# New order lists for both ends of a fused attention and adapter kernel

## The chip, the cores and the metric

The kernel runs on one core of one Trainium2 chip. The metric is the time of one execution on the device in microseconds. The profile is of one further execution; its span counts from the first to the last instruction. Five engines work in parallel[...]: TensorE (PE: matmuls and transposes), VectorE (DVE), ScalarE (ACT: exp, tanh, copies), GpSimd (POOL) and SyncE (SP: issues DMA transfers).[...]

## The reference: what is computed

For each of 4 batches, 12288 queries of 128 channels attend to 768 keys. The keys are 4 x 4 means of a 384 x 32 image, times a weight matrix, and serve as values too. Each of the 49152 output rows then gets a top-2 mixture of 8 low-rank adapters (rank 16).

```python
B, C, Hh, Ww = (4, 128, 384, 32)
kv_pool = kv.reshape(B, H // r, r, W // r, r, C).mean(axis=(2, 4))   # r = 4
k = v = kv_pool.reshape(B, -1, C) @ w_sr
s = (q @ k.transpose(0, 2, 1)) / np.sqrt(C)
a = np.exp(s - s.max(-1, keepdims=True)); a /= a.sum(-1, keepdims=True) + 1e-09
x = (a @ v).reshape(B * S, D)
logits = x @ w_gate                        # 8 experts, the two largest kept
for e in range(E):                         # w: softmax over the two kept logits
    z = x[mask] @ A[e]; delta[mask] += w[mask, k, None] * (z @ B[e])
return x + delta
```

## The kernel before: the parts concerned

The 49152 queries are 96 chunks of 512 (`T`), 24 per batch. The 768 keys of a batch are six tiles of 128, handled in three blocks `h` of two tiles. A chunk goes through these stages, named as in the order lists:

```python
def scores(k, r):       # "sc k r": one third of the keys: 2 matmuls of 512 columns on PE, 1 exp on ACT
    ps = ps_s.tile([P, 2, T], FP32, tag="sg", name="sg")            # PSUM, 2 buffers of 2 banks
    for i in range(2):
        mm(ps[:, i], kfT[b][:, 2 * r + i], rhs, start=True, stop=True)
    keep(nc.scalar.activation(em[k][:, 2 * r:2 * r + 2], ps, AF.Exp, bias=0.0, scale=scale))

def attend(k, s):       # "at k s": 128 queries against all keys: 6 matmuls of 137 columns into acc
    acc[k] = ps_a.tile([P, S, 256], FP32, tag="acc", name="acc")    # PSUM, 1 buffer of 2 banks
    for j in range(J):
        mm(o, em[k][:, j, s * P:(s + 1) * P], vx[b][:, j], start=(j == 0), stop=(j == J - 1))

def normalize(k):       # "nm k": DVE, reciprocal and product of all 4 x 136 columns
# "tp k": DVE, 4 maxima;  "ro"/"ga": GpSimd and one tanh on ACT, the gates of the experts
# "tt kx kh V|A": PE transposes x of chunk kx and the gated h of chunk kh, one copy on DVE or ACT
# "dn k": PE, x times A (4 matmuls);  "ge k": DVE, h times gates;  "up k": PE, times B (4 matmuls)
# "fi k": DVE adds x, SP stores 256 KB
# "ca k" / "pd k": instead of "fi", ACT copies the sum out of PSUM and GpSimd adds x
# tail forms with PSUM of their own choice: xt, cx (transpose x, copy), hb, ht, ch (the same of h),
# dn2, ge2, db, up2, af (add and store); a pair "0 2" or "2 4" means half a chunk
```

`ps_m` ("mb") holds everything else in PSUM: 2 buffers of one bank. `keep(...)` fixes the program order. The first loads and the preparation of the first batch:

```python
keep(nc.scalar.dma_start(w_sr_sb, w_sr))
keep(nc.scalar.dma_start(w_gate_sb, moe_w_gate))
load_q(0, 0, GC * S)                       # 1 MB: queries of chunks 0 to 3
for h in range(3):                         # 6 MB: keys, 24 transfers of 256 KB
    for r in range(4):
        for x in range(2):
            load_kv(0, h, r, x)
for m in range(GC):
    load_q(1, m * S, m * S + S)            # 4 x 256 KB: queries of chunks 4 to 7
...
def pair_step(h, r, x):                    # "ad": DVE adds two of the four image rows
    u, v = (kvr[b, h][:, r + i, x] for i in range(2))
    keep(adder.tensor_tensor(u, u, v, op=ALU.add))
# "ky h half": PE transposes the 16 sums of the block in fp32, adding them up in PSUM;
#              DVE scales by 1/16.  "k2 h": times w_sr -> keys kfT.  "va h": values vx.
# "tq g m e":  the first 8 query chunks are transposed on PE (fp32), 4 transposes and a copy
def first_casts(watch):                    # "cs1": GpSimd waits for the last query load, then starts
    keep(nc.gpsimd.tensor_copy(late, watch))   # the casts of later queries in DRAM
    for g in range(2, 4):
        cast_q(g)
```

Chunks 0 to 13 follow a list written out, chunks 14 to 71 a regular slot, and chunks 72 to 95 a second list:

```python
def slot(k):
    ...
    o.append(f"sc {k} 0")
    o += [f"nm {k - 2}", f"tt {k - 6} {k - 7} V", f"sc {k} 1", f"up {k - 8}", f"fi {k - 8}",
          f"at {k - 1} 0", f"tp {k - 2}"]
    o += [f"sc {k} 2", f"dn {k - 6}", f"ge {k - 6}"]
    o += [f"at {k - 1} {s}" for s in range(1, S)]
```

The head list begins "ad 0 0; tq 0 0 A; ad 0 1; ad 0 2; cs1; tq 0 1 A; ad 0 3; ky 0 0; ...". In the tail list the slot's order goes on, with the open stages of older chunks brought in two at a time between chunks 72 and 78. From chunk 93 on the half forms are used.

Of the kernel before, what the change touches and what calls it, by code (L numbers as in the profile page):

```python
# [20 lines left out]
def kernel(  # L21
# [10 lines left out]
    nc = tc.nc  # L32
# [74 lines left out]
    def turn_q(g, m, engine):  # L107
        if g not in qT:
            qT[g] = qpool.tile([P, GT], BF16, tag="qT", name="qT")
        ps = mtile([P, S, P], name="qT_ps")  # L110
        for i in range(S):
            mm(ps[:, i], q_f[g][:, m * S + i], id_f, is_transpose=True,
               start=(i == 0), stop=(i == S - 1))
        o = qT[g][:, m * T:(m + 1) * T].rearrange("p (s t) -> p s t", s=S)
        if engine is nc.scalar:
            keep(nc.scalar.copy(o, ps))
        else:
            keep(nc.vector.tensor_copy(o, ps))
# [6 lines left out]
    load_q(0, 0, GC * S)  # L125
    for h in range(3):
        for r in range(4):
            for x in range(2):
                load_kv(0, h, r, x)
    for m in range(GC):  # L130
        load_q(1, m * S, m * S + S)
    b_f = const.tile([P, C], FP32)
    keep(nc.sync.dma_start(b_f, moe_B.rearrange("e r c -> (e r) c")))
    a_f = const.tile([P, P], FP32)
    keep(nc.sync.dma_start(a_f, moe_A.rearrange("e c r -> c e r")))


    warm = const.tile([P, 1], FP32)
    nc.vector.memset(warm, 0.0)
    keep(nc.scalar.activation(warm, warm, AF.Exp, bias=0.0, scale=1.0))  # L140
    id_f = const.tile([P, P], FP32)
    make_identity(nc, id_f)
    id_bf = const.tile([P, P], BF16)
    nc.vector.tensor_copy(id_bf, id_f)
    wext = const.tile([P, VC], FP32)
    nc.vector.tensor_copy(wext[:, 0:C], w_sr_sb)
    wT_ps = mtile([P, C], name="wT_ps")
    mm(wT_ps, w_sr_sb, id_f, is_transpose=True, start=True, stop=True)
    wT = const.tile([P, C], FP32)
    nc.vector.tensor_copy(wT, wT_ps)  # L150
    w2_ps = mtile([P, E], name="w2_ps")
    mm(w2_ps, wT, w_gate_sb, start=True, stop=True)
    nc.vector.tensor_copy(wext[:, C:VC], w2_ps)


    kfT, vx = {}, {}

    def prepare(b, adder):
# [3 lines left out]
        def pool_step(h, step, lo, hi):  # L162
            t = kvr[b, h]
            if step < 3:
                u, v = t[:, 0].rearrange("p g c -> p (g c)"), t[:, step + 1].rearrange("p g c -> p (g c)")
            else:
                w = 2 * C if step == 3 else C
                u, v = t[:, 0, :, 0:w], t[:, 0, :, w:2 * w]
                keep(adder.tensor_tensor(u, u, v, op=ALU.add))
                return  # L170
            keep(adder.tensor_tensor(u[:, lo:hi], u[:, lo:hi], v[:, lo:hi], op=ALU.add))  # L171

        def pair_step(h, r, x):
            u, v = (kvr[b, h][:, r + i, x] for i in range(2))
            keep(adder.tensor_tensor(u, u, v, op=ALU.add))

        for h in range(3):
            if adder is nc.vector:
                sums.append([lambda h=h, r=r, x=x: pair_step(h, r, x)
                             for r in (0, 2) for x in range(2)])  # L180
                continue
# [5 lines left out]
        def keys(h, half=None):  # L187
            if h == 0 and half != 1:
                st["kpT"] = prep.tile([P, J, P], FP32, tag="kpT", name="kpT")
                kfT[b] = per_b.tile([P, J, P], BF16, tag="kfT", name="kfT")  # L190
            kpT = st["kpT"]
            if half != 1:
                st["ps"] = mtile([P, 2, P], name="kpT_ps")
            ps = st["ps"]
            if adder is nc.vector:
                parts = [(r, i, c) for r in (0, 2) for i in range(2) for c in range(4)]
            else:
                parts = [(0, i, 0) for i in range(2)]
            for n, (r, i, c) in enumerate(parts):
                if half is not None and r // 2 != half:  # L200
                    continue
                mm(ps[:, i], kvr[b, h][:, r, i, c * C:(c + 1) * C], id_f, is_transpose=True,
                   start=(n == 0), stop=(n == len(parts) - 1))
            if half == 0:
                return
            keep(nc.vector.tensor_scalar(kpT[:, 2 * h:2 * h + 2], ps, 1.0 / 16.0, None,
                                         op0=ALU.mult))

        def keys2(h):
            kpT = st["kpT"]  # L210
            ps = mtile([P, 2, P], name="kfT_ps")
            mm(ps, w_sr_sb, kpT[:, 2 * h:2 * h + 2], start=True, stop=True)
            keep(nc.vector.tensor_copy(kfT[b][:, 2 * h:2 * h + 2], ps))  # L213

        def values(h):
# [7 lines left out]
            if adder is not nc.vector:  # L223
                st["vb", h] = prep.tile([P, 2, C], BF16, tag="vb", name="vb")
                keep(nc.vector.tensor_copy(st["vb", h], ps[:, :, 0:C]))
# [8 lines left out]
        for h in range(3):  # L234
            for f in (keys, keys2, values) if adder is nc.vector else (keys, values, turn):
                rest.append(lambda h=h, f=f, **how: f(h, **how))
# [17 lines left out]
    def attend(k, s):  # L254
        b = k // NB
        if k not in acc:
            acc[k] = ps_a.tile([P, S, 256], FP32, tag="acc", name="acc")
        o = acc[k][:, s, 0:VE]
        for j in range(J):
            mm(o, em[k][:, j, s * P:(s + 1) * P], vx[b][:, j], start=(j == 0), stop=(j == J - 1))  # L260
# [11 lines left out]


# [16 lines left out]
    def route(k0):  # L290
        n = size[k0] * S
        eng = nc.gpsimd if k0 > 1 else nc.vector
# [74 lines left out]
    def bank(pool):  # L367
# [20 lines left out]
    def turn_x(k, pool):  # L388
        xT[k] = quad(bank(pool).bitcast(BF16), pool)
        xb = xn[k].bitcast(U16)[:, :, 1::2].bitcast(BF16)  # L390
        for s in range(S):
            mm(xT[k][:, s // 2, s % 2], xb[:, s, 0:C], id_bf, is_transpose=True,
               start=(s % 2 == 0), stop=(s % 2 == 1))

    def copy(engine, o, i):
        keep(nc.scalar.copy(o, i) if engine == "A" else nc.vector.tensor_copy(o, i))  # L396

    def fetch_x(k, engine):
        sb = run.tile([P, S, P], BF16, tag="tt1", name="tt1")
        copy(engine, four(sb), xT[k])  # L400
        xT[k] = sb
# [3 lines left out]
    def hold_h(k, pool):  # L405
        hps[k] = quad(bank(pool).bitcast(BF16), pool)

    def turn_h(k, lo=0, hi=S):
        for s in range(lo, hi):
            mm(hps[k][:, s // 2, s % 2], hg[k][:, s], id_bf, is_transpose=True,  # L410
               start=(s % 2 == 0), stop=(s % 2 == 1))

    def fetch_h(k, lo=0, hi=S, engine="A"):
        if lo == 0:
            hgT[k] = run.tile([P, S, P], BF16, tag="tt1", name="tt1")
        copy(engine, part(four(hgT[k]), lo, hi), part(hps[k], lo, hi))

    def hold_acc(k, pool="sg"):
        acc[k] = bank(pool)
# [3 lines left out]
    def attend_part(k, lo, hi):  # L423
        for s in range(S):
            for j in range(lo, hi):
                mm(acc[k][:, s, 0:VE], em[k][:, j, s * P:(s + 1) * P], vx[k // NB][:, j],
                   start=(j == 0 and s % 2 == 0), stop=(j == J - 1 and s % 2 == 1))

    def down_into(k, pool):
        hp[k] = quad(bank(pool), pool)  # L430
        for s in range(S):
            mm(hp[k][:, s // 2, s % 2], xT[k][:, s], a_bf, start=(s % 2 == 0), stop=(s % 2 == 1))

    def gate_part(k, lo, hi):
        if lo == 0:
# [3 lines left out]
        keep(nc.vector.tensor_tensor(  # L439
            part(four(hg[k]).rearrange("p a b (e r) -> p a (b e) r", e=E), lo, hi),  # L440
            part(four(hp[k]).rearrange("p a b (e r) -> p a (b e) r", e=E), lo, hi),
            part(g4, lo, hi).unsqueeze(3).broadcast_to([P, (hi - lo) // 2, 2 * E, RK]), op=ALU.mult))

    def hold_d(k, pool):
        dp[k] = quad(bank(pool), pool)

    def up_part(k, lo, hi):
        for s in range(lo, hi):
            mm(dp[k][:, s // 2, s % 2], hgT[k][:, s], b_bf, start=(s % 2 == 0), stop=(s % 2 == 1))
# [5 lines left out]
    def add_here(k, lo, hi, queue="SP"):  # L455
        osb = opool.tile([P, S, C], FP32, tag="osb", name="osb")[:, 0:hi - lo]
        keep(nc.vector.tensor_tensor(osb.rearrange("p (a b) c -> p a b c", b=2),
                                     part(four(dp[k]), lo, hi),
                                     part(four(xn[k][:, :, 0:C]), lo, hi), op=ALU.add))
# [57 lines left out]
    def plan(b):  # L517
        if b not in plans:
            plans[b] = prepare(b, nc.gpsimd if b else nc.vector)
# [3 lines left out]
        "tq": lambda g, m, e: turn_q(g, m, nc.scalar if e == "A" else nc.vector),  # L523
        "ad": lambda h, i: plan(0)[0][h][i](),
        "ky": lambda h, half: plan(0)[1][3 * h](half=half),
        "k2": lambda h: plan(0)[1][3 * h + 1](),
        "va": lambda h: plan(0)[1][3 * h + 2](),
        "cs": lambda: first_casts(kvr[0, 2][:, 3, 1, 0:1]),
        "cs1": lambda: first_casts(q_f[1][:, GC * S - 1, 0:1]),
# [10 lines left out]
        "xt": turn_x, "cx": lambda k, e="A": fetch_x(k, e), "hb": hold_h, "ht": turn_h, "ch": fetch_h,  # L540
        "o95": hold_acc, "pt": attend_part, "dn2": down_into, "ge2": gate_part,
# [4 lines left out]
    def follow(order):  # L546
        for item in order.replace("\n", " ").split(";"):
            what, *at = item.split()
# [31 lines left out]
ad 0 0; tq 0 0 A; ad 0 1; ad 0 2; cs1; tq 0 1 A; ad 0 3; ky 0 0; tq 0 2 V; ky 0 1; k2 0; ad 1 0; va  # L580
0; sc 0 0; tq 0 3 A; lq 2; sc 2 0; ad 1 1; ad 1 2; ad 1 3; ky 1 0; sc 1 0; ky 1 1; ad 2 0; sc 3 0;
k2 1; ad 2 1; va 1; sc 3 1; ad 2 2; sc 0 1; ky 2 0; sc 2 1; ad 2 3; kv 1 0 0; ky 2 1; sc 1 1; k2 2;
tq 1 0 V; sc 0 2; va 2; cab; sc 4 2; tq 1 1 V; at 0 2; kv 1 0 1; sc 1 2; at 0 1; sc 4 0; at 0 0; at
# [89 lines left out]
```

## Time and profile before

| | us |
|---|---|
| time, median of 3 | 393.8 (393.69 to 394.21) |
| span of the profiled execution | 392.3 |
| PE busy | 376.4 |
| VectorE busy | 325.3 |
| ScalarE busy | 298.0 |
| GpSimd busy | 205.0 |

The page's part 5 gives the durations of the main pieces (line, engine, operation, output<-input, shape and count; then busy us and mean ns of one; then the idle time of the engine just before them and what ended it):

```profile
L252 ACT ACTIVATE em<-sg 128x1024 f16<-128x1024 f32 x288 | 280.9, 1023 | 75.6 <-PE sg L68 74.7
L268 DVE TENSOR_TENSOR xn<-acc,rinv 128x544 f32<-128x544 f32 x95 | 68.8, 725 | 3.3
L349 DVE TENSOR_TENSOR hg<-h_ps,gw 128x512 bf16<-128x512 f32 x93 | 64.2, 690 | 7.0 <-PE h_ps L68 0.2
L335 DVE COPY tts<-tt_ps 128x1024 bf16<-128x1024 bf16 (+1 forms) x93 | 61.6, 663 | 2.6 <-PE tt_ps L68 1.6
L362 DVE TENSOR_TENSOR osb<-d_ps,xn 128x512 f32<-128x512 f32 x89 | 61.2, 690 | 0.0
```

Matmuls overlap in PE's pipeline, so their mean ns (379 for a score matmul) is longer than the distance from one to the next; that distance has to be read from the timeline or from the chain of waits.

### The profile page before, as it was taken

The page shows a single profiled execution, that of the slowest core. Times are in us where ns is not written, and L with a number is a line of the kernel's source. Part 1 is how long each engine was busy: PE and PEld are TensorE (multiplying, and loading weights), DVE is VectorE, ACT ScalarE, POOL GpSimd, SP SyncE. Part 2 cuts the span into 40 slices and gives each one's busy share as a digit, 9 for nine tenths or more (in the row PEclk, how much of TensorE's full clock was granted, in tenths as well). Part 3 has the DMA queues.
Part 4 walks back from the last instruction along what each step waited for, and adds up shares of the span by engine and source line. Part 5 has one row for each costly group of instructions (what it writes and reads, how often), then busy time and mean ns, then how long its engine had stood idle before and what let it go on. Part 6 is the DMA issues. An engine that isn't in the chain of part 4 may idle for free.

```text
span 392.3 us, 11714 instructions
## 1 busy us (share of the span) xinstructions
PE 376.4 (96%) x4589; PEld 302.3 (77%) x4589; DVE 325.3 (83%) x950; ACT 298.0 (76%) x375; POOL 205.0 (52%) x473
## 2 busy tenths in 40 slices
PE   3999999999999999999999999999999899999993
PEld 2767878888887888878888878888786678878882
DVE  2666769989888889888988988989887888888885
ACT  2378988787687787787777877877788787877873
POOL 0010479998331778587432677877524235444443
PEclk9999999999999999999999999999999999999997
DMA  8998969974596989885489999957644566573213
GB/s 296 367 266 222 210 237 245 264 173 136 140 304 145 298 206 342 183 190 135 108 217 256 297 257 295 187 139 134 156 142 110 154 157 148 144 159 105 79 60 136
DMA packets 71464, 76.47 MB, mean 195 GB/s; under 512 B 49936, under 2 KB 50704, under 8 KB 70928
## 3 DMA queue, kind: packets, MB, share of 16 engines
q1 hardware_dynamic: 70272, 63.98, 56.4%
q0 software_dynamic: 704, 11.54, 17.1%
q8 instruction: 36, 0.59, 0.6%
q10 hardware_dynamic: 432, 0.20, 0.2%
q14 instruction: 20, 0.16, 0.1%
HBM read 50.53 MB, written 36.70 MB: 222 GB/s over the span
## 4 chain that ended last, share of the span: by engine, by line
PE 85%; DMA 5%; SPq 3%; DVE 3%; POOL 2%; issue 1%; ACT 1%; ACTq 0%; DVEq 0%; POOLq 0%
PE acc L68 33%; PE sg L68 29%; PE tt_ps L68 10%; PE h_ps L68 5%; PE d_ps L68 5%; SPq L98 3%; DMA qT<-qbf 2%; DMA w_sr_sb<-in_w_sr_dram 1%; DMA kvr<-in_kv_dram 1%; PE v_ps L68 1%; PE kpT_ps L68 1%; DVE tts L335 1%; POOL kvr L171 1%; DVE xn L268 1%; ACT tt L396 0%
## 5 line engine op out<-in xcount | busy, mean ns | idle before, releaser
L252 ACT ACTIVATE em<-sg 128x1024 f16<-128x1024 f32 x288 | 280.9, 1023 | 75.6 <-PE sg L68 74.7
L68 PE MATMUL sg<-qT,kfT 128*128 128x512 bf16 x576 | 170.4, 379 | 0.4 <-DVE kfT L213 0.2
L68 PE MATMUL acc<-vx,em 128*128 128x137 f16 x2280 | 168.1, 223 | 0.0
L68 PEld LDWEIGHTS <-em 128*128 128x128 f16 x2304 | 146.1, 98 | 3.1 <-DVE xn L268 1.1
L68 PEld LDWEIGHTS <-tts 128*128 128x128 bf16 x740 | 56.1, 98 | 43.9 <-issue 2.8
L171 POOL TENSOR_TENSOR kvr<-kvr 128x512 f32<-128x512 f32 x54 | 67.5, 1274 | 13.1 <-DVE tts L335 13.1
L268 DVE TENSOR_TENSOR xn<-acc,rinv 128x544 f32<-128x544 f32 x95 | 68.8, 725 | 3.3
L349 DVE TENSOR_TENSOR hg<-h_ps,gw 128x512 bf16<-128x512 f32 x93 | 64.2, 690 | 7.0 <-PE h_ps L68 0.2
L335 DVE COPY tts<-tt_ps 128x1024 bf16<-128x1024 bf16 (+1 forms) x93 | 61.6, 663 | 2.6 <-PE tt_ps L68 1.6
L362 DVE TENSOR_TENSOR osb<-d_ps,xn 128x512 f32<-128x512 f32 x89 | 61.2, 690 | 0.0
L299 POOL TENSOR_TENSOR over<-xn,srt 128x64 f32<-128x64 f32 (+1 forms) x116 | 30.4, 283 | 56.0 <-DVE srt L286 56.0
L313 POOL TENSOR_TENSOR gw<-th,over 128x64 f32<-128x64 f32 (+1 forms) x58 | 17.0, 294 | 64.0 <-ACT th L311 63.7
L68 PEld LDWEIGHTS <-kfT 128*128 128x128 bf16 x576 | 45.6, 98 | 2.9 <-DVE kfT L213 1.0
L264 DVE RECIPROCAL rinv<-acc 128x4 f32<-128x4 f32 x95 | 17.4, 183 | 35.1 <-PE acc L68 34.5
L68 PEld LDWEIGHTS <-xn 128*128 128x128 bf16 x384 | 28.9, 98 | 20.0 <-DVE xn L268 0.4
L68 PE MATMUL d_ps<-b_bf,tts 128*128 128x128 bf16 x364 | 35.1, 219 | 1.6 <-DVE tts L335 1.1
L68 PE MATMUL h_ps<-a_bf,tts 128*128 128x128 bf16 x372 | 36.0, 219 | 0.3 <-ACT tts L333 0.3
L68 PE MATMUL tt_ps<-id_bf,xn 128*128 128x128 bf16 x372 | 35.8, 219 | 0.0
L68 PE MATMUL tt_ps<-id_bf,hg 128*128 128x128 bf16 x368 | 35.6, 219 | 0.0
L286 DVE MAX8 srt<-xn 128x8 f32<-128x8 f32 x380 | 34.3, 154 | 0.0
L68 PEld LDWEIGHTS <-hg 128*128 128x128 bf16 x384 | 25.8, 98 | 1.7 <-issue 0.4
L305 POOL TENSOR_SCALAR over<-over 128x64 f32<-128x64 f32 (+1 forms) x58 | 19.5, 336 | 5.3
(83 smaller groups left out, 208.5 us busy)
## 6 DMA issues: line engine op xcount, KB each, us to landing
out_dram<-osb SPq DMA_DIRECT2D x94, 256.0 KB, 3.6
kvr<-in_kv_dram SPq DMA_DIRECT2D x36, 512.0 KB, 6.1
qbf<-in_q_dram POOLq DMA_DIRECT2D x22, 512.0 KB, 6.2
kvr<-in_kv_dram SPq DMA_DIRECT2D x24, 256.0 KB, 5.1
qf<-in_q_dram SPq DMA_DIRECT2D x1, 1024.0 KB, 5.1
qf<-in_q_dram SPq DMA_DIRECT2D x4, 256.0 KB, 5.3
out_dram<-osb SPq DMA_DIRECT2D x3, 128.0 KB, 2.3
qT<-qbf SPq DMA_TRANSPOSE x22, 5.5
```

Of the source, the lines that this page charges most:

```text
L68: return keep(nc.tensor.matmul(*a, **k))
L171: keep(adder.tensor_tensor(u[:, lo:hi], u[:, lo:hi], v[:, lo:hi], op=ALU.add))
L252: keep(nc.scalar.activation(em[k][:, 2 * r:2 * r + 2], ps, AF.Exp, bias=0.0, scale=scale))
L264: keep(nc.vector.reciprocal(ri, acc[k][:, :, VC]))
L268: keep(nc.vector.tensor_tensor(x, acc[k][:, :, 0:VC], ri.unsqueeze(2).broadcast_to([P, S, VC]), op=ALU.mult))
L286: keep(nc.vector.max(srt[k0][:, m, s], xn[k][:, s, C:VC]))
L299: keep(eng.tensor_tensor(d, lg, so[:, :, i].unsqueeze(2).broadcast_to([P, n, 8]), op=ALU.subtract))
L305: keep(eng.tensor_scalar(mask, mask, 0.0, None, op0=ALU.is_ge))
L313: keep(eng.tensor_tensor(w[:, 0:n], th, mask, op=ALU.mult))
L335: keep(nc.vector.tensor_copy(sb[:, lo:hi], ps[:, lo:hi]))
L349: keep(nc.vector.tensor_tensor(hg[k].rearrange("p s (e r) -> p (s e) r", e=E), hp[k].rearrange("p s (e r) -> p (s e) r", e=E), gw[k0][:, m ...
L362: keep(nc.vector.tensor_tensor(osb, dp[k], xn[k][:, :, 0:C], op=ALU.add))
```

## The change

It changes what runs before chunk 14 and after chunk 71; the slot between is kept. Its aims: the first keys are loaded ahead of the queries, so that scores can begin sooner. PE multiplies zeros until data comes[...]. Both ends follow new lists in which scores run further ahead and late stages are cut into halves or go to another engine. Where two halves of a PSUM tile lie in different banks, the dependence between them is dropped.

```diff
-    load_q(0, 0, GC * S)
-    for h in range(3): ... load_kv(0, h, r, x)          [cut: 24 transfers of 256 KB]
-    for m in range(GC):
-        load_q(1, m * S, m * S + S)
+lkv 0 1 -; lkv 0 0 -; lf 1 1 2; lkv 0 3 -; lkv 0 2 -; lf 0 0 2; lf 0 2 4; lkv 1 2 -; lkv 1 3 -; lkv
+1 0 -; lkv 1 1 1; lkv 1 1 0; lkv 2 3 -; lkv 2 2 -; lkv 2 0 0; lkv 2 1 0; lkv 2 0 1; lkv 2 1 1; lf 1
+2 3; lf 1 0 1; lf 1 3 4; lab
     [lkv h r x: keys, "-" is a whole row set of 512 KB; lf g lo hi: query chunks; lab: adapters]
+    idle = const.tile([P, T], BF16)
+    keep(nc.vector.memset(idle, 0.0))
+    def spin(n):
+        ps = mtile([P, T], name="spin_ps")
+        for i in range(n):
+            mm(ps, idle[:, 0:P], idle, start=True, stop=True)
+    spin(11)
     [the weights' first steps move into weights(), "init" in the list]
+    def use(key, lo, hi, inst):
+        ...
+                tc.declare_no_dep(inst.ins, other.ins, reason="other PSUM bank")
+    def turn_k(h, half, x):               # "ky h half x": 4 transposes of a summed pair,
+        rows = [2 * half] if (h, 2 * half, x) in summed else [2 * half, 2 * half + 1]   # else 8
     [7 pair sums in the list instead of 12; "kc" scales, on ACT or DVE; k2, va, tq likewise]
+    def normalize_half(k, h):             # "nh k h": one bank's reciprocal and product
+    def attend_part(k, lo, hi):           # "pt k lo hi": keys lo..hi of all 512 queries, as exps come
-        eng = nc.gpsimd if k0 > 1 else nc.vector
+        eng = nc.gpsimd
-        "cs1": lambda: first_casts(q_f[1][:, GC * S - 1, 0:1]),
+        "cs": lambda w: first_casts(q_f[1][:, 15, 0:1]),
     [head list, its beginning]
+kb 1 mb; kb 0 sg; init; ad 0 2; ky 0 0 1; ky 0 0 0; tq 1 1 V mb; db 1 sg; ky 0 1 1; cs k; xb 3 mb;
+ky 0 1 0; kb 2 mb; kc 0 A; tq 0 0 A acc; tq 0 1 A sg; k2 0 sg A; lq 2; tq 0 2 V mb; tq 0 3 V mb; ad
+1 2; va 0 acc A; sc 5 0; kv 1 0 0; sc 0 0; ad 1 1; ky 1 1 1; ky 1 1 0; sc 1 0; sc 3 0; ky 1 0 0; ky
+1 0 1; ad 2 3; pt 0 0 2; ad 2 2; kc 1 A; ad 2 0; k2 1 mb A; ad 2 1; sc 2 0; va 1 mb V; sc 5 1; ky 2
+1 1; sc 1 1; ky 2 1 0; sc 3 1; ky 2 0 0; sc 0 1; ky 2 0 1; kv 1 0 1; kv 1 0 2; kc 2 V; tq 1 2 A mb;
+sc 2 1; k2 2 mb V; sc 6 1; va 2 mb V; kv 1 0 3; sc 0 2; tq 1 3 V mb; pt 0 2 4; sc 3 2; pt 0 4 6; sc
+1 2; tq 1 0 A mb; xb 1 mb; sc 2 2; nm 0; pt 1 0 2; hb 0 mb; ...
     [tail list, its end]
+95 acc; at 94 2; at 94 3; ch 90 0 2 A; ch 90 2 4 A; ga 93; db 92 acc; tt - 89 A; at 94 0; ge2 91 0
+4; at 94 1; hd 95 mb; tp 95; tt 92 - A; nh 94 1; nh 94 0; ro 95; dn2 93 0 4; ht 88 0 4; ge2 93 0 4; ...
+af 91 0 4 SP; af 92 0 2 SP; af 92 2 4 ACT; af 95 0 4 SP; db 94 acc; up2 94 0 4; fi 94
     [10 output adds of the tail go by "ca" and "pd" instead of 2; most attends go by parts ("pt")]
```

## The prediction

> **What bounds the kernel now.** I read the page's first two parts first (busy shares, then the 40 slices), then the chain of waits, then stage windows, and last the timeline of both ends.
>
> ```profile
> PE 376.4 (96%) x4589; PEld 302.3 (77%) x4589; DVE 325.3 (83%) x950; ACT 298.0 (76%) x375; POOL 205.0 (52%) x473
> PE   3999999999999999999999999999999899999993
> PEclk9999999999999999999999999999999999999997
> DMA  8998969974596989885489999957644566573213
> ```
>
> The reader is to see that TensorE (PE) is full from the second slice to the last but one, at full granted clock. Only the ends can give time back. How full it is inside comes from the cadence of the chain of waits:
>
> ```profile
> 324.33 1.08 PE acc L68 x18
> 327.96 1.08 PE acc L68 x18
> 331.59 1.08 PE acc L68 x18
> ```
>
> One chunk of 512 queries passes every 3.63 us. The pieces between are 1.44 us of attend (24 matmuls, 0.060 each), three score pairs of 0.43, 0.45 of transposes, and 0.22 each for down and up; they sum to 3.62 us. So the middle has no idle PE, and 96 x 3.63 = 348.5 of the 392.3 us are pure throughput. The rest is what the ends and the key preparation cost. The stage windows (start:end, length, then busy us and instructions of PE, PEld, DVE, ACT, POOL, clock, DMA share, GB/s) show where:
>
> ```profile
> 6.00:15.00 9.00, 7.88 (x39) 6.79 (x40) 5.32 (x12) 1.17 (x2) 0.00 (x0) 1.00 1.02 369
> 15.00:26.10 11.10, 10.48 (x64) 6.86 (x63) 7.32 (x16) 8.25 (x9) 0.42 (x2) 1.00 1.00 347
> 26.10:40.00 13.90, 13.90 (x152) 11.00 (x153) 9.15 (x38) 12.06 (x14) 0.97 (x2) 1.00 0.90 216
> ...
> 290.00:320.00 30.00, 28.10 (x356) 21.92 (x354) 24.48 (x65) 23.98 (x32) 10.68 (x40) 1.00 0.52 132
> 320.00:380.00 60.00, 60.00 (x767) 48.45 (x765) 52.19 (x151) 48.73 (x66) 26.21 (x104) 1.00 0.46 125
> 380.00:392.30 12.30, 6.16 (x82) 4.72 (x78) 7.40 (x26) 5.56 (x14) 4.40 (x10) 0.81 0.30 110
> ```
>
> Until 26.1 us the DMA share is 1.0: the 8.4 MB of first loads bind. From 320 to 380 PE does 767/60 = 12.8 matmuls per us; from 290 to 320 only 356/30 = 11.9, so 30 - 356/12.8 = 2.2 us are lost there; after 380, 82/12.8 = 6.4 us of work take 12.3. The timeline of the start gives the cold clock and the moment from which PE is full:
>
> ```profile
> 9.21 1.97 PE L68 MATMUL kpT_ps<-id_f,kvr 128*128 128x128 f32 x8
> ...
> 15.39 1.02 ACT L252 ACTIVATE em<-sg 128x1024 f16<-128x1024 f32 x1 [5.38 <-PE sg L68]
> ...
> 16.06 1.04 PE L68 MATMUL kpT_ps<-id_f,kvr 128*128 128x128 f32 x8
> ...
> 22.23 1.42 DVE L175 TENSOR_TENSOR kvr<-kvr 128x512 f32<-128x512 f32 x2 [0.54 <-DMA kvr<-in_kv_dram]
> ...
> 24.88 0.70 PE L68 MATMUL kfT_ps<-kpT,w_sr_sb 128*128 128x256 f32 x2
> ...
> 26.10 0.60 PE L68 MATMUL sg<-qT,kfT 128*128 128x512 bf16 x2
> ```
>
> The same eight fp32 transposes took 1.97 us at 9.2 and 1.04 at 16.1. The third key block's data is there at 22.2 to 22.9, and its scores start at 26.10. The window 26.1:40 contains 26 score matmuls (5.6 us), 96 attends (5.8), 14 small bf16 ones (0.8) and 16 fp32 ones (1.9): 14.1 us for 13.9. So PE is truly full from 26.1 on. **The head costs whatever steady work is still undone at that moment.**
>
> [...]The trace's 128 KB stores land 2.3 us after issue, the 256 KB ones after 3.6 under load. [...]The trace: an add of 512 columns takes 0.69 us, one of 256 columns 0.41.[...]
>
> **Part 1: order of the first loads.** Before, 1 MB of queries goes ahead of the keys. After, two of the four row sets of the first key block, a 256 KB query chunk (chunk 5), the other two rows, and then the 1 MB. The first block is complete after 2.25 MB instead of 3 MB, about 0.75 MB/0.39 = 2 us sooner (rate: 380 to 393 GB/s in the saturated 2 us windows). But before the last key piece stand 7.25 MB instead of 7.0: 0.65 us later. Set against this are whole-row transfers (one 0.6 us issue for 512 KB instead of 0.65 per 256 KB, where the rate dipped to 334 to 356), perhaps 0.5 us, and one pair sum instead of two after the last piece, 0.7. I expect the third key block's scores at 26.3 to 27.0, so about where they were. The watch of the query casts is the same last query column as before: nothing.
>
> **Part 2: spin.** 11 matmuls of 512 columns at the cold rate (2 x 0.215 = 0.43) are 4.7 us, from about 1.2 to 5.9, before w_sr lands (6.0 before). It costs nothing and makes the first transposes 0.11 apart instead of 0.22: 28 of them save 3 us of PE time in a stage where data binds. Alone it is worth little at the end.
>
> **Part 3: head list.** PE work listed ahead of the first third-block score (0.11 per fp32 transpose, 0.45 per query turn, 0.65 per key projection, 0.5 per value projection, 0.43 per score pair): before 48 transposes 5.3 + 5 turns 2.25 + 3 projections 2.0 + 2 values 1.0 + 8 pairs 3.45 + weights 1.0 = 15 us. After: 68 transposes 7.5 (five pair sums fewer on VectorE, 20 transposes more on PE) + 6 turns 2.7 + 2.0 + 3 values 1.55 + 11 pairs 4.7 + one attend part 0.5 + 1.0 = 20 us. Steady work moved ahead of the point: 3 pairs 1.3 + 1 turn 0.45 + 1 value 0.5 + 0.5 = 2.7 us. From this go the later point (0.2 to 0.9) and ScalarE: its six second-block exps can start only near 21.5 and run 0.93 to 1.0 apart plus a 0.59 query copy, so the score buffers (two) free up about 0.5 us late. Net head gain 2.7 - 0.7 - 0.6 = 1.4 us.
>
> **Part 4: tail list and halves.** From the middle's end (291 us) both lists do the same matmuls, about 95 us by the rates above. VectorE, by the row durations: before 26 normalizes 23.5, 25 maxima 9.1, 24 double copies 16.6, gates 20.9, adds 21.0, the rest 1.2 = 92.3 us. After: 17 whole and 18 half normalizes 25.8, maxima and late routes 12.9, copies 14.1, gates 21.2, adds 15.7 = 89.7, because ten output adds go through ScalarE (copy 0.59) and GpSimd (1.27). ScalarE rises from about 78 to 86 us (72 exps at 0.93, 26 tanh at 0.12, some 30 copies), which still fits. Scores run several chunks ahead (seven em buffers), so PE should not hit the 2.2 us of stalls at 290 to 320, where the catch-up doubled VectorE's work. At the very end it is the other way round: after the last attend, before had 11 groups of four matmuls (2.5 us) and 6.9 us to the last add. After, 20 groups (4.5 us) and on VectorE two half normalizes 1.2, maxima 0.7, 4 gates 2.8, eight adds 5.0 (one chunk in halves) = 9.7 us. The last attend thus comes 2.2 + 2.0 us sooner and is followed by 2.8 us more: +1.4. If VectorE's total counts (2.6 less), up to +3. The last store has 256 KB and a full add, -0.5. I take +2.6 - 0.5 = 2.1 us, plus 0.5 for finer bank waits.
>
> **Sum.** 1.4 + 2.1 + 0.5 = 4.0 us of 393.8: 389.8 us.
>
> **Rivals.** (a) Nearly nothing: the head stays bound by the 8.4 MB, whose last key piece comes 0.65 us later, and the tail turns PE stalls into a VectorE backlog. For it: the DMA share of 1.0 up to 25 us, and 9.7 us of VectorE work behind the last attend; 392.5 to 394. (b) Near the ideal: PE full from 6 us to the end. All PE work is 348.5 + 7.7 (key preparation of three batches, 9 steps each at about 0.28 us, by the slots of 3.74 to 4.15 us in the chain) + 15.6 (the first batch: 7.5 + 8 turns 3.6 + 2.0 + 1.55 + 1.0) = 371.8 (rounded); + 6 at the start + about 5 at the end = 383. For it: the middle shows that such lists hold PE at 100%. Against it: 20 us of work ahead of a point at 26.5 leave 0.5 us of slack. I would give it 386 at best. (c) Slower: a fixed order on in-order engines, with long runs through one acc buffer and score buffers lent to gates, meets a late cast or transposed load, and stalls stack up; 395 to 398. Against it: the list before was of the same kind and ran without PE idle from 26 to 70.
>
> **Range and chances.** Head 0 to 2.7, tail 0 to 4.5: the range is 386.6 to 393.0. Over 2% means below 385.9, which needs (b) nearly whole: 0.10. Slower by over 2% means above 401.7: 0.02. The rest, 0.88, within 2%.
>
> **What would show it.** First exp at 13 to 14 us instead of 15.4; transposes 0.11 apart from the start; the first third-block score near 26.5 and PE full after it. In the window 290:320 PE back at 12.8 matmuls per us. At the end, VectorE nearly without gaps after the last attend while PE has them. I am wrong if the first third-block score comes later than 27.5 (rival a), if PE shows gaps between 27 and 70 (c), or if the time from the last attend to the end is under 10 us although seven chunks' adds are open (b).

## The result, and the profile after

| | before | after |
|---|---|---|
| time, median of 4 | 393.76 us (393.69 to 394.21) | 388.93 us (388.78 to 389.29) |
| span of the profiled execution | 392.3 us | 387.5 us |

The ratio of the times is 0.9876, with a 95% interval of 0.9859 to 0.9893: 1.2% faster, 4.8 us. The prediction was 389.8 us (386.6 to 393.0).

From the page of the changed kernel, busy time of each engine and two of the 40-slice rows:

```profile
PE 378.9 (98%) x4620; PEld 303.8 (78%) x4620; DVE 313.5 (81%) x973; ACT 308.3 (80%) x401; POOL 211.0 (54%) x474
...
PE   7899999999999999999999999999999999999994
...
DMA  7998997975596999985579989856745665532245
```

VectorE has 12 us less to do than before, ScalarE 10 us and GpSimd 6 us more. PE has 2.5 us more, in a span 4.8 us shorter. In the PE row, the 7 in the first slice is mostly the zeros.

The stage windows of the changed kernel (start:end, length, then busy us and instructions of PE, PEld, DVE, ACT, POOL, clock, DMA share, GB/s):

```profile
6.00:15.00 9.00, 7.24 (x60) 6.47 (x59) 2.76 (x6) 1.84 (x5) 0.00 (x0) 1.00 1.02 388
15.00:26.10 11.10, 10.78 (x78) 7.89 (x76) 5.15 (x10) 9.63 (x13) 0.06 (x1) 1.00 0.94 348
...
290.00:320.00 30.00, 30.00 (x350) 22.80 (x348) 22.61 (x86) 29.20 (x38) 9.60 (x31) 1.00 0.59 124
...
380.00:387.50 7.50, 2.46 (x32) 1.73 (x30) 3.94 (x8) 2.31 (x5) 0.85 (x3) 0.87 0.66 247
```

The DMA share is still about 1 up to 26 us, so the first loads fill the queues as before. But PE does 138 instructions between 6 and 26.1 us instead of 103. Between 290 and 320 us PE no longer idles at all. After 380 us only 32 matmuls are left (82 before), and the DMA share of that stretch is 0.66 instead of 0.30: what is left is mostly stores.

The timeline of the head of the changed kernel (start, duration, engine, line, operation, output<-input, shape, count; in brackets the idle time before it and what ended it):

```profile
6.93 1.95 PE L68 MATMUL sg<-id_f,kvr 128*128 128x128 f32 x16
...
10.74 0.69 DVE L195 TENSOR_TENSOR kvr<-kvr 128x512 f32<-128x512 f32 x1 [3.46 <-DMA kvr<-in_kv_dram]
...
15.33 1.94 ACT L319 ACTIVATE em<-sg 128x1024 f16<-128x1024 f32 x2
...
24.20 0.69 DVE L195 TENSOR_TENSOR kvr<-kvr 128x512 f32<-128x512 f32 x1 [0.56 <-DMA kvr<-in_kv_dram]
...
27.64 0.59 PE L68 MATMUL sg<-qT,kfT 128*128 128x512 bf16 x2
```

Row by row: the first 16 transposes take 1.95 us. The last rows of the first key block are there at 10.74. The first exp starts at 15.33 (15.39 before). The last key piece is there at 24.20 (22.2 to 22.9 before), and the first third-block score starts at 27.64 (26.10 before). So the first exp did not move, and the third-block score moved back by 1.5 us. These marks differ from one execution to the next: in seven traces with this head, this one among them, the first exp starts between 14.74 and 15.65, the third-block score between 27.11 and 28.00.

Where the time went is read from a mark that both kernels share. The first two key transposes of batch 1 stand in the unchanged middle, in the slot of chunk 14 (tile view; after the count come the durations in ns, min/median/max, then the first and last start in us). Before:

```profile
L68 PE MATMUL kpT_ps<-id_f,kvr x2: 273/276/280, 70.3 to 70.4; 128*128 128x128 f32 x2
```

After:

```profile
L68 PE MATMUL kpT_ps<-id_f,kvr x2: 272/277/282, 69.3 to 69.4; 128*128 128x128 f32 x2
```

The changed kernel passes it 1.05 us sooner (unrounded starts). The last key preparation of the middle comes at 284.4 instead of 285.5, so the middle gave nothing. **In these two executions 1.05 of the 4.8 us come from the head and 3.75 from the tail.** The seven traces with this head and the bank rule pass the mark between 68.7 and 69.6, the two with the head of before at 70.1 and 70.3. So the head's share is about 1 us, and a difference of some tenths between two single traces says nothing.

The end of the changed kernel, in the timeline (SPq is the engine that issues the stores):

```profile
375.34 0.88 PE L68 MATMUL acc<-vx,em 128*128 128x137 f16 x12
...
380.84 3.65 SPq L554 DMA_DIRECT2D out_dram<-osb  x5
...
383.45 0.69 DVE L551 TENSOR_TENSOR osb<-acc,xn 128x512 f32<-128x512 f32 x1
```

The last attend ends at about 376.2. Before, the last attend matmuls were these, and ended at 382.2:

```profile
381.56 0.64 PE L68 MATMUL sg<-vx,em 128*128 128x137 f16 x8
```

From the last attend to the end it takes 11.3 us instead of 10.1.

### The profile page after: what moved, and what is told of

Same layout as the page of the kernel before. It is cut to its first block, busy times and chain, and to the rows that moved or that the text cites. A ratio compares the mean times of both kernels' runs of the same rounds, so it can differ in the third digit from the quotient of the medians.

```text
span 387.5 us, 11812 instructions
## 1 busy us (share of the span) xinstructions
PE 378.9 (98%) x4620; PEld 303.8 (78%) x4620; DVE 313.5 (81%) x973; ACT 308.3 (80%) x401; POOL 211.0 (54%) x474
## 4 chain that ended last, share of the span: by engine, by line
PE 82%; DMA 8%; POOL 5%; DVE 1%; ACT 1%; issue 1%; SPq 0%; POOLq 0%; DVEq 0%; ACTq 0%
PE acc L68 32%; PE sg L68 29%; PE tt_ps L68 8%; DMA kvr<-in_kv_dram 6%; PE h_ps L68 4%; PE d_ps L68 3%; PE tail_ps L68 3%; DMA qT<-qbf 2%; POOL osb L562 1%; PE v_ps L68 1%; POOL over L380 1%; PE kpT_ps L68 1%; POOL gw L394 1%; ACT em L319 1%; POOL gw L395 1%
## 5 line engine op out<-in xcount | busy, mean ns | idle before, releaser
L68 PEld LDWEIGHTS <-tts 128*128 128x128 bf16 x660 | 49.2, 98 | 31.8 <-issue 0.2
L337 DVE TENSOR_TENSOR xn<-acc,rinv 128x544 f32<-128x544 f32 x83 | 60.1, 724 | 3.2 <-DVE rinv L333 0.3
L416 DVE COPY tts<-tt_ps 128x1024 bf16<-128x1024 bf16 (+1 forms) x83 | 53.9, 651 | 4.8 <-PE tt_ps L68 4.6
L430 DVE TENSOR_TENSOR hg<-h_ps,gw 128x512 bf16<-128x512 f32 x58 | 40.1, 691 | 4.5
L443 DVE TENSOR_TENSOR osb<-d_ps,xn 128x512 f32<-128x512 f32 x58 | 40.1, 691 | 0.0
L68 PE MATMUL tt_ps<-id_bf,xn 128*128 128x128 bf16 x344 | 33.3, 219 | 0.0
L68 PE MATMUL tt_ps<-id_bf,hg 128*128 128x128 bf16 x316 | 30.4, 219 | 0.0
L68 PE MATMUL h_ps<-a_bf,tts 128*128 128x128 bf16 x264 | 25.5, 219 | 0.0
L68 PE MATMUL d_ps<-b_bf,tts 128*128 128x128 bf16 x260 | 25.1, 219 | 0.0
```

Source lines behind the costliest of these rows:

```text
L68: return keep(nc.tensor.matmul(*a, **k))
L337: keep(nc.vector.tensor_tensor(x, acc[k][:, :, 0:VC], ri.unsqueeze(2).broadcast_to([P, S, VC]), op=ALU.mult))
L416: keep(nc.vector.tensor_copy(sb[:, lo:hi], ps[:, lo:hi]))
L430: keep(nc.vector.tensor_tensor(hg[k].rearrange("p s (e r) -> p (s e) r", e=E), hp[k].rearrange("p s (e r) -> p (s e) r", e=E), gw[k0][:, m ...
L443: keep(nc.vector.tensor_tensor(osb, dp[k], xn[k][:, :, 0:C], op=ALU.add))
```

## The experiments

Each ratio is to the kernel before, timed on the same chip, with its 95% interval. The changed kernel was run again beside some of the later experiments, as a control: 389.18 us, 0.9884 [0.9869, 0.9899].

### Head alone, tail alone

The changed kernel with the tail list of before (in the new stage forms):

```diff
- nm 70; sc 72 1; xb 66 mb; db 71 mb; hd 73 mb; lq 19; sc 72 2; ...        [tail list of the change]
+ lq 19; sc 72 0; ga 68; nm 70; tt 66 65 V; sc 72 1; up 64; fi 64; ...     [tail list of before]
```

> The changed kernel with the tail list of before (in the new forms of the tail stages). Theory: the two ends are separated by a middle in which PE is full, so their gains add; the marker at the first slot came 1.04 us sooner, so this is 1.0 us faster than before: 392.7, and 3.8 slower than the changed kernel. Rival (the head's lead only moves a wait from the start to the tail): no faster than before, 393.5 to 394.

And the kernel before with the tail list, the stages and the bank rule of the change:

```diff
- lq 19; sc 72 0; ga 68; nm 70; tt 66 65 V; sc 72 1; up 64; fi 64; ...
+ nm 70; sc 72 1; xb 66 mb; db 71 mb; hd 73 mb; lq 19; sc 72 2; ...
```

> The kernel before with the tail list and tail stages of the changed kernel. Theory: 3.7 us faster than before, 390.1, and the window 290 to 320 us shows PE without idle time. Rival (the tail needs the head's lead, or the head's list is most of the gain): under 2 us faster, above 391.8.

| | us | ratio | gain |
|---|---|---|---|
| head alone | 393.03 | 0.9982 [0.9975, 0.9990] | 0.7 us |
| tail alone | 390.47 | 0.9917 [0.9904, 0.9931] | 3.2 us |

The product of the two ratios is 0.990, the changed kernel has 0.988. The two gains sum to 3.9 of its 4.5 to 4.8 us; the rest lies within the intervals, so no dependence between the two parts is shown. One oddity stands in the way of a closer sum: in the head-alone kernel the time is 2.1 us longer than the span, in the other kernels 1.8. By the medians of the spans the head alone gives 0.9 us instead of 0.7. Why isn't known. In the head-alone kernel, the stage window of the old catch-up shows the stalls again:

```profile
290.00:320.00 30.00, 28.10 (x360) 22.11 (x358) 24.73 (x67) 24.20 (x32) 11.26 (x43) 1.00 0.52 135
```

PE is busy for the same 28.10 us as before the change. In the tail-alone kernel it is busy for all 30. So the idle time belonged to the old tail list, whatever the head does.

### The bank rule taken away

A buffer of two PSUM banks is one tile. The change drops the dependence between instructions that touch different banks of it. Here it is kept everywhere:

```diff
         for other, theirs in users.setdefault(key, []):
-            if not mine & theirs:
+            if False:
                 tc.declare_no_dep(inst.ins, other.ins, reason="other PSUM bank")
```

> The changed kernel with the dependences between halves in different PSUM banks kept; same order on every engine. Theory of the prediction: the finer waits are worth 0.5 us, so 389.4. Rival (the lists rest on them, each half waits for the other): 391 or more. Other rival (nothing waits there): within 0.1 us of the changed kernel.

Measured: 392.38 us, 0.9963 [0.9951, 0.9976]. Losing the rule costs 3.2 to 3.5 us, against an estimate of 0.5. The rival (the lists rest on the rule) was right. The timeline of this kernel shows how:

```profile
33.82 0.89 PE L68 MATMUL acc<-vx,em 128*128 128x137 f16 x12
...
34.96 0.44 DVE L351 TENSOR_TENSOR xn<-acc,rinv 128x272 f32<-128x272 f32 x1
...
35.45 0.88 PE L68 MATMUL acc<-vx,em 128*128 128x137 f16 x12 [0.74 <-DVE xn L351]
```

In the changed kernel the same 24 matmuls are one row:

```profile
33.92 1.61 PE L68 MATMUL acc<-vx,em 128*128 128x137 f16 x24
```

Half a chunk is attended into one bank. With the rule, the second half goes on at once into the other bank while VectorE normalizes the first. Without it, the second half waits until VectorE has read the first: a gap of 0.74 us on PE in the middle of a chunk. PE is idle for 1.04 us between 28 and 70 us here, and never in the changed kernel. The mark of chunk 14 is passed at 70.5, so the head's whole gain is gone (1.2 us; 1.6 from the first third-block score on, which comes at 27.30 here). From that mark's counterpart at 285 us to the end, this kernel needs 105.0 us; the changed one needs 103.1, the kernel before 106.8. The tail thus loses 1.9 of its 3.7 us. The lists were written for the rule; what lists made for whole-buffer waits would give wasn't tried.

### Ten adds back on VectorE

```diff
- ca 65; ... pd 65; ... ca 69; ... pd 69; ...    [10 adds: ScalarE copies, GpSimd adds]
+ fi 65; ... fi 69; ...                          [VectorE adds; PE's order as before]
```

> The changed kernel with the ten output adds of the tail that ScalarE and GpSimd share put back on VectorE, PE order unchanged; VectorE gets 10 x 0.65 = 6.5 us more and ScalarE 10 x 0.5 us less between 285 and 384. Theory (VectorE is the second bound of the tail, 89.7 of some 95 us): 3 to 5 us slower, 392 to 394, with PE waiting for VectorE in the tail. Rival (PE alone binds, the spread of the adds is free choice): within 1 us, below 390.

Measured: 392.96 us, 0.9981 [0.9973, 0.9990], 4.0 us slower than the changed kernel. Windows of this kernel from the middle's end on:

```profile
285.00:376.00 91.00, 88.70 (x1102) 69.66 (x1100) 74.77 (x261) 76.49 (x104) 30.00 (x117) 1.00 0.50 122
376.00:391.20 15.20, 9.38 (x143) 8.19 (x140) 11.28 (x34) 7.91 (x19) 5.13 (x21) 0.95 0.42 157
```

And of the changed kernel:

```profile
285.00:376.00 91.00, 90.98 (x1165) 73.51 (x1163) 74.61 (x266) 83.39 (x120) 43.18 (x135) 1.00 0.48 126
376.00:387.50 11.50, 6.27 (x88) 4.92 (x85) 7.90 (x19) 5.88 (x14) 4.33 (x14) 0.92 0.49 185
```

VectorE works the same 74.7 us up to 376 in both. With ten more adds in its order it gets less of the rest done: PE idles 2.3 us, and at 376 us VectorE still has 11.28 us to do instead of 7.90. Two rows from the waits of this kernel after 284 us say where PE stood (who waited, for what: us, times, longest):

```profile
PE acc L68 <- DVE xn L337: 1.2, 2, 0.8
...
PE tt_ps L68 <- DVE osb L443: 0.7, 1, 0.7
```

Attends waited twice, 1.2 us in all, until a normalize had emptied their PSUM buffer, and a transpose waited 0.7 us behind an output add. The changed kernel has neither row in this stretch. From the key preparation at 284 us to the end this kernel takes 107.2 us, the changed one 103.1: the whole loss is in the tail. VectorE is the second bound of the tail, although its busy share there is only 82%: what counts is that it is late at single points.

### Spin left out

```diff
-    spin(11)
```

> The changed kernel without the 11 matmuls on zeros. Theory: the first key block's second half lands only at 10.7 us and PE idles 1.4 us before it, so a cold clock until about 10 us costs 0 to 0.3 us at the end: 388.9 to 389.2. Rival (the warm clock carries the head's gain): 1 us or more, above 389.9; eight fp32 transposes in 1.9 us instead of 1.0 at 7 us are expected in either case.

Measured: 389.62 us, 0.9894 [0.9879, 0.9910]; no difference from the changed kernel can be told. In the timeline of this kernel the first transposes run at half speed, and then at full:

```profile
6.38 3.68 PE L68 MATMUL sg<-id_f,kvr 128*128 128x128 f32 x16 [0.52 <-DMA kvr<-in_kv_dram]
...
10.33 1.47 PE L68 MATMUL sg<-id_f,kvr 128*128 128x128 f32 x12
```

The 16 take 3.68 us instead of 1.95. In the changed kernel PE then waited 1.37 us for the block's last rows, until 10.69; here it comes to them at 10.33 and finds them there. The 1.7 us are taken out of a wait for data. The zeros don't secure the full speed either: in the run with ten adds back on VectorE, which has them, the same 16 transposes took 3.65 us, and its mark of chunk 14 (69.1) is no later than that of others. The clock column of the windows doesn't show this; it says 1.00 for both runs while the transposes run at half speed, and also for the kernel before from 9 to 11 us, where eight took 1.97 us. So the cold and the warm clock of the prediction and of the expectation are the author's names for two measured durations, 3.68 and 1.95 us for 16 transposes; what sets them isn't shown.

### The order of the first loads

Queries of chunks 0 to 3 (1 MB) ahead of the keys, as before the change:

```diff
- lkv 0 1 -; lkv 0 0 -; lf 1 1 2; lkv 0 3 -; lkv 0 2 -; lf 0 0 2; lf 0 2 4; lkv 1 2 -; ...
+ lf 0 0 2; lf 0 2 4; lkv 0 1 -; lkv 0 0 -; lf 1 1 2; lkv 0 3 -; lkv 0 2 -; lkv 1 2 -; ...
```

> The changed kernel with the 1 MB of queries of chunks 0 to 3 loaded ahead of the first keys, all else the same. Theory: the first key block is complete 2 to 2.6 us later, the last key piece at the same time; the eleven exps ahead of the first third-block score then run into each other on ScalarE and cost 0.5 to 1 us: 389.4 to 389.9. Rival (only the last key piece counts): within 0.2 us of the changed kernel. Other rival (early first keys carry the head): the whole head gain goes, 390 or more.

Keys in 256 KB transfers instead of whole rows:

```diff
- lkv 0 1 -; lkv 0 0 -; ...
+ lkv 0 1 0; lkv 0 1 1; lkv 0 0 0; lkv 0 0 1; ...      [9 transfers of 512 KB -> 18 of 256 KB]
```

> The changed kernel with each whole-row key transfer (512 KB, 4 KB per partition row) split into two of 256 KB (2 KB per partition row), order kept. After 7 us the changed kernel moved 411 GB/s, the one before with half rows 376. Theory (the size of the pieces sets the rate): the last key piece lands about 1.5 us later than 24.2, and the end comes 1 to 1.4 us later: 390 to 390.3. Rival (the depth of the queue or chance set the rate): rate over 400 GB/s, time within 0.2 us of the changed kernel.

The one query chunk between the first key rows moved behind them, in the loads and in the list:

```diff
- lkv 0 1 -; lkv 0 0 -; lf 1 1 2; lkv 0 3 -; lkv 0 2 -; ...
+ lkv 0 1 -; lkv 0 0 -; lkv 0 3 -; lkv 0 2 -; lf 1 1 2; ...
- ky 0 0 0; tq 1 1 V mb; db 1 sg; ky 0 1 1; cs k; xb 3 mb; ky 0 1 0; kb 2 mb; ...
+ ky 0 0 0; db 1 sg; ky 0 1 1; cs k; xb 3 mb; ky 0 1 0; tq 1 1 V mb; kb 2 mb; ...
```

> The changed kernel with the early 256 KB query chunk loaded behind the whole first key block instead of in its middle, and its transposes moved behind that block's. Theory (the first block's completion sets the head, as with the queries first): the block is complete 0.5 to 0.7 us sooner and the end 0.3 to 0.6 us: 388.3 to 388.7. Rival (the query's transposes fill a gap that now stays idle, and the last piece lands no sooner): 388.8 to 389.4.

Times in us, rates from windows of each trace; in the first row the time is the control's and the rest is from the first trace of the changed kernel (the control's own trace: 10.28, 14.99, 24.16, 69.6, and 332 and 406 GB/s):

| | time, ratio | first block complete | first exp | last key piece | mark of chunk 14 | GB/s 4 to 7, 7 to 24 us |
|---|---|---|---|---|---|---|
| changed kernel | 389.18, 0.9884 | 10.74 | 15.33 | 24.20 | 69.3 | 303, 407 |
| queries first | 390.92, 0.9927 [0.9914, 0.9940] | 13.15 | 17.83 | 23.34 | 71.2 | 399, 398 |
| half rows | 390.86, 0.9923 [0.9910, 0.9935] | by 11.55 | 16.27 | 25.03 | 70.1 | 234, 392 |
| query after keys | 389.09, 0.9884 [0.9871, 0.9898] | 9.41 | 15.09 | 23.86 | 68.9 | 393, 396 |

Queries first: the last key piece comes 0.9 us sooner, and the kernel is still 1.7 us slower. So the last piece alone doesn't set the head; the early start of the first block does. PE has some 4 us of work between a complete block and its first score (13.15 to 17.19 in this run, 10.69 to 14.70 in the changed kernel), and after that its list leaves it hardly a gap: it is busy for 11.93 of the 12 us from 16 to 28 in this run, and for 11.68 in the changed kernel. The loss is more than the theory gave and takes more than the head's gain with it: the mark of chunk 14 (71.2) is later than before the change (70.3), where the queries also came first. The new list has no work on these queries to fill the wait for the keys, so this run tests the load order under this list only.

Half rows cost 1.7 us, by the ratios, and the last key piece came later, as the theory said (0.8 us instead of 1.5). But the loss of the head is there before that piece. The start of PE in this run:

```profile
7.78 3.13 PE L68 MATMUL sg<-id_f,kvr 128*128 128x128 f32 x16 [1.29 <-DMA kvr<-in_kv_dram]
...
10.69 1.06 PE L68 MATMUL tail_ps<-id_f,qf 128*128 128x128 f32 x4
...
11.55 1.61 PE L68 MATMUL sg<-id_f,kvr 128*128 128x128 f32 x12
```

At 234 GB/s the first rows come late. PE waits 1.29 us for them, and its next 20 transposes run mostly at half speed (3.13 and 1.06 us instead of 1.95 and 0.60) although the zeros stand ahead of them (here the clock column shows it: 0.50 from 9 to 11 us). It comes to the block's second half at 11.55 instead of 10.69, and from 13 to 28 us it is busy for 14.81 of 15 us. The first exp, the third-block score (28.47) and the mark are then all 0.8 or 0.9 us later than in the changed kernel. The late last piece costs PE under 0.2 us in this stretch. How much the late rows cost and how much the half speed, no run separates; nor is it shown where the rest of the 1.7 us goes. The rate of 392 GB/s lies below that of all traces with the same order of loads in whole rows (402 to 410), but two other orders of whole rows had 398 and 396.

Query after keys: the first block is complete 1.3 us sooner, and nothing comes of it. Between the block and the first score PE's list now holds 20 query transposes instead of 16, besides a projection and the values, and PE waits for the queries of chunk 0:

```profile
11.75 0.66 PE L68 MATMUL acc<-id_f,qf 128*128 128x128 f32 x4 [0.44 <-DMA qf<-in_q_dram]
```

The rate of 4 to 7 us is higher without the chunk between the rows, but that wasn't on the path.

### The end mended, three ways

The last output add comes alone (383.45 above), as a whole chunk, after PE has run dry. Halving it looked like free gain. First try, in halves and with GpSimd's gates of chunk 94 ahead of its add of chunk 88:

```diff
- up2 93 2 4; ht 91 2 4; pd 88; ga 94; ...     db 94 acc; up2 94 0 4; fi 94
+ up2 93 2 4; ht 91 2 4; ga 94; pd 88; ...     db 94 mb; up2 94 0 2; af 94 0 2 SP; up2 94 2 4; af 94 2 4 ACT
```

> The changed kernel with two edits of the last steps: GpSimd does the last chunk's gates ahead of the output add of chunk 88 (1.27 us), and the last chunk's up product, add and store go in halves on two queues. Theory: the chain at the end goes through GpSimd's gates and the last whole add and 256 KB store, so 0.3 to 0.6 us are gained: 388.3 to 388.6. Rival (VectorE is full from 376 to 384 us and binds alone): two halves cost it 0.1 more, no gain, 388.8 to 389.1.

Second try, with the two-bank buffer and a seventh output buffer:

```diff
- db 94 mb; up2 94 0 2; ...
+ db 94 acc; up2 94 0 2; ...
-    opool = ... bufs=6
+    opool = ... bufs=7
```

> The mended tail again, with its two faults taken away: the last chunk's halves stay in the two-bank acc buffer, so that the second product need not wait for the first add, and there are 7 output buffers instead of 6. The gates of chunk 94 still go ahead of the add of chunk 88. Theory: the waits of 2.0 and 0.9 us of the last attempt are gone and 0.3 to 0.6 us are gained on the changed kernel: 388.3 to 388.7. Rival (VectorE is full to the end[...]): 388.8 to 389.3.

Third, the halves alone, GpSimd's order as in the change:

```diff
- ga 94; pd 88
+ pd 88; ga 94
```

> The changed kernel with only the last chunk's product, add and store in halves (two-bank buffer, 7 output buffers); GpSimd's order as in the change. Theory: what cost 1.5 us in the last mended tail is the later add of chunk 88, whose store then goes out at 381.8 instead of 380.6 and holds up all later ones in the one in-order store queue, while the stores fill the DMA engines to the end; the halves alone change little: 388.9 to 389.5. Rival (the halves and their second queue cost it): 390 or more.

| | us | ratio |
|---|---|---|
| first try | 390.67 | 0.9921 [0.9907, 0.9934] |
| second try | 390.67 | 0.9926 [0.9913, 0.9938] |
| halves alone | 389.32 | 0.9894 [0.9877, 0.9910] |

Both tries lost 1.5 us, and both theories with them. In the first, the buffer has one bank, so the second half waited 2.00 us for the first half's add, and the first half's add waited 0.93 us for an output buffer. The two waits, in the first try:

```profile
383.64 0.42 DVE L551 TENSOR_TENSOR osb<-tail_ps,xn 128x256 f32<-128x256 f32 x1 [0.93 <-DMA out_dram<-osb]
...
384.12 0.27 PE L68 MATMUL tail_ps<-b_bf,tt 128*128 128x128 bf16 x2 [2.00 <-DVE osb L551]
```

The second try removed the wait of 2.00 and left 0.49 us of the other: its last VectorE add ends at 384.33, as in the control (384.34), yet its span is 389.2 against 387.7. What differs is in SyncE's timeline. Second try:

```profile
381.76 0.33 SPq L563 DMA_DIRECT2D out_dram<-osb  x1
382.19 2.55 SPq L554 DMA_DIRECT2D out_dram<-osb  x5
```

Control:

```profile
380.62 0.33 SPq L563 DMA_DIRECT2D out_dram<-osb  x1
381.05 3.66 SPq L554 DMA_DIRECT2D out_dram<-osb  x5
```

L563 is the store of chunk 88, which GpSimd now adds 1.1 us later. SyncE issued the stores in the same order in both runs: the five behind it start at 382.19 instead of 381.05, 1.1 us later too, and then all move at once: the DMA engines run at 386 to 398 GB/s from 383 to 386 in the second try, after only 107 and 154 GB/s in the microseconds 381 to 383 (301 and 313 in the control). In the last whole microsecond of the transfers, the second try and then the control (the last two numbers are DMA share and GB/s):

```profile
386.00:387.00 1.00, 0.00 (x0) 0.00 (x0) 0.00 (x0) 0.00 (x0) 0.00 (x0) 0.74 0.69 239
...
386.00:387.00 1.00, 0.00 (x0) 0.00 (x0) 0.00 (x0) 0.00 (x0) 0.00 (x0) 1.00 0.04 14
```

The third run tests it: with only GpSimd's order restored the loss is gone, so that order is its cause, and the halves neither help nor harm by more than the uncertainty. How the later store costs 1.5 us is shown in part. The data of the stores end some 0.6 us later in the second try (386.6 against 386.0). The other 0.9 us pass between the last data and the end of the kernel: 2.6 us against 1.7, and 2.2 in the third run, whose loss is gone. What lengthens that stretch stays open. None of the runs beats the changed kernel by more than its uncertainty.

## Why the prediction was right, step by step

- **Part 1, loads.** "First block about 2 us sooner": it came at 10.74 (10.06 to 10.37 in the other six traces with this head), at most 1.5 us sooner than before the change, where the block's last two pair sums are these:

```profile
10.79 1.46 DVE L175 TENSOR_TENSOR kvr<-kvr 128x512 f32<-128x512 f32 x2 [1.17 <-DMA kvr<-in_kv_dram]
```

The rate taken was 380 to 393 GB/s; between 4 and 7 us it was 303. That the last key piece would come later was right, but its size was off: 1.3 to 2.0 us later instead of 0.65 less some 0.5. The third-block score came at 27.64, past the 27.5 that I had named as a sign of rival (a); in four of the other six traces it came before 27.5.
- **Part 2, spin.** Right that it is worth nothing at the end. The transposes were 0.11 us apart from the start in six of the seven traces with this head, but not in the seventh. The premise, that work on PE ahead of them brings the full speed, isn't shown. The run without spin had half speed from 6.38 to about 9.9 us and then full speed; but the seventh trace had zeros from 1.21 to 6.09 us, then no pause of over 0.4 us, and half speed up to about 10.8.
- **Part 3, head list.** "Steady work moved ahead of the point: 2.7 us" less the delay. The accounting held: 2.7 - 1.54 (the delay measured) = 1.16, and the mark moved by 1.05. It holds in the other traces too. From the first third-block score to the mark of chunk 14 it is 44.2 us in both traces with the old head (26.10 to 70.3, and 25.93 to 70.1), and 41.6 or 41.7 in all eleven with the new head or a variant of it and the bank rule: 2.5 to 2.6 us were moved ahead. The term "0.2 to 0.9" for the delay was too small, and the further 0.6 for ScalarE can't be seen. The delay was read from the loads, but what sets the point is PE's own list: with the queries first PE is hardly idle after 13.18 us, and its third-block score starts 16.4 us later, at 29.58; in the changed kernel 16.95 us lie between 10.69 and 27.64. All waits in between, those for late keys included, are then worth some 0.5 us there. Rival (a) was right about the late point but not about its worth, because work had been moved ahead. "First exp at 13 to 14 us" was wrong: 15.33.
- **Part 4, tail.** The stalls at 290 to 320 are gone, as said. The marker given for it, 12.8 matmuls per us, was badly chosen: it is 350/30 = 11.7, with PE full. In that window 62 of the matmuls are 512-column scores (41 before), because scores run ahead. A count is no measure where the mix changes. The last attend was to come 1.4 + 4.2 = 5.6 us sooner and came 6.0 sooner. After it, 2.8 us more were expected and 1.2 measured: VectorE was given 9.7 us there and has 7.9 from 376 us on.
- **The step that failed: "plus 0.5 for finer bank waits".** Measured, this term is 3.2 to 3.5 us, 1.2 in the head and 1.9 in the tail. Without it the head's list is worth nothing and the tail's about 1.85 us. The prediction took the rule as a refinement; it is the condition for halves. The head's 1.4 and part of the tail's gain were booked on the lists, where the bank rule is what makes those lists run without gaps. So it is partly luck that the sum came near: the head was put 0.35 us too high, and the tail with the rule at 2.6 instead of 3.75.
- **VectorE as the tail's second bound, with its ten adds moved away:** shown, 4.0 us by itself. The bank rule cost 1.9 in the tail. Together that is 5.9, more than the tail gained: each loss is measured with the other part in place, and they overlap.
- **Rival (b), near the ideal,** needed the time after the last attend below 10 us. It is 11.3. What stands there now is no engine: from 384 to 386 us almost only stores move, at 390 and 320 GB/s, and the last 1.5 us hold nearly no data.
- **Rival (c)** didn't come: PE has no gaps from 27 to 70 us.
- **The range.** Its upper end doesn't follow from its terms: head 0 and tail 0 are 393.8, not 393.0.

Not tried: a kernel with neither the bank rule nor the moved adds, which would show how much the two share, and the kernel before with the bank rule alone.

## What to carry to other kernels

When a stage is cut in halves that share a buffer of several banks, first see which waits are kept between the halves: here whole-buffer dependences cost 1.2 us in the head, all that the reordering had brought there. Load first the data with the longest chain of work behind it, not the data that is used first; a later last piece may be cheaper than a later first one (here the last key piece 0.9 us sooner, with the first block 2.4 us later, made the kernel 1.7 us slower). Take the same mark from several traces before reading tenths of a microsecond: here seven traces of one head lay 0.9 us apart. At the end of a kernel look at the order in which stores are issued before shortening the last arithmetic: here one store that came 1.1 us later held up the five issued behind it.

## What was unexpected of the hardware

- A 64 KB weight load, issued first on ScalarE's queue, was usable at 2.54 to 2.68 us wherever key rows were issued beside it, in 512 KB transfers or in 256 KB ones. It came at 6.0 beside the 1 MB query load of before, and at 5.35 beside two query transfers of 512 KB. So the size of the transfers beside it isn't what delays it; what it is stays open.
- In the same order of loads, whole image rows moved at 402 to 410 GB/s (7 to 24 us, nine traces), the rows in halves at 392. The kernel before, with halves throughout and another order, had 374.
- With one query chunk of 256 KB between the key rows the rate at 4 to 7 us was 303 to 374 GB/s in nine traces. With the chunk behind the rows it was 393, in one trace. Why, and why it varies so, isn't settled.
- In the run without spin, PE did only three small matmuls before its first key transposes at 6.38 us. 16 of these fp32 transposes took 3.68 us, and the next 12 took 1.47.
